# Pooled sums of the first batch by accumulated products on TensorE, with a new order of steps

## The chip, the cores and the metric

The kernel runs on one core of a Trainium2 chip (trn2). The metric is the time of one execution in device microseconds; a value for a kernel is the median of its runs. Engines are named as the profile names them: PE is TensorE (PEld its weight loads), DVE is VectorE, ACT is ScalarE, POOL is GpSimd, SP is SyncE, which issues all the transfers here.

## The reference, cut to what matters

Eight batches, eight heads, 576 tokens, head size 64. Attention has two parts that are added. The pooled part works on means over four tokens:

```python
q_d = q.reshape(B, H, Sd, factor, D).mean(axis=3)     # factor = 4, Sd = 144
k_d = k.reshape(B, H, Sd, factor, D).mean(axis=3)
v_d = v.reshape(B, H, Sd, factor, D).mean(axis=3)
out_up = np.repeat(sm_attn(q_d, k_d, v_d), factor, axis=2)
# local part: full q, k, v with a mask |i - j| < 4, softmax, times v
x = (out_up + out_local).transpose(0, 2, 1, 3).reshape(B * S, H * D)    # 4608 x 512
h = x @ w_in                                     # 512 x 1024
solu = h * softmax(h)
ln = (solu - mean) / sqrt(var + 1e-6) * g_ln
out = ln @ w_out                                 # 1024 x 512
```

All inputs of the attention are float32; the two weight matrices come as 64-bit floats.

## The kernel before, in words

Heads are worked in pairs (two heads of 64 fill 128 partitions), so a batch has four pairs. For each pair q and k are brought to the layout "head size on partitions, tokens along the row" (`qT`, `kT`, 128x576), and the sums over four neighbouring tokens are formed from it (`qd_flat`, `kd`, 128x144; the mean's factor is folded into the softmax scale).

The first two batches (`EarlyBatch`) get that layout from TensorE: a load puts 6 consecutive tokens of a head into each of 96 partitions, and twelve products with an identity matrix (6 token positions, 2 heads; tiles `qp`, `kp`, line L557) turn them into PSUM. One copy, on ACT or DVE (L263 or L265), moves 128x576 to `qT` or `kT`, and `sums` (L419, a DVE reduction over groups of four) makes `qd_flat` and `kd`. The later batches use DVE transposes instead (L463, L467), followed by the same reductions.

From there: `Pooled` per pair (products `sd`, L788; row maxima `mxd`, L795; exponentials `pd`, L803; scaling by the reciprocal sum, L812; transposes `pdt`, L823; products `po`, L844), `Local` per two windows of 64 tokens (scores `sc`, L600 and L607; L620 to L645; transposes `plt`, L655; products `xp`, L665), or `PairOfLocals` in the later batches. Their results add up in `x`.

The feed-forward network runs over 36 tiles of 128 tokens. `xhl` splits x in two float32r parts (`xh` on ACT, L1017; `xl`, L1020); `ffn_in` makes `h` from 24 matmuls of 512 columns (L862), then row maximum `nmx` (DVE, L870), exponential (ACT, L874), product (DVE, L877), small steps on POOL (L882 to L926). The result goes to memory and comes back in turned blocks (`u`, `v`; L910, L942), is turned by DVE (L963), split into `uh` and `ul` (L969, L972), and `ffn_out` makes `o` from 24 more matmuls (L986). The weights are converted once from 64-bit floats, in 16 pieces (`w`, L364 to L412), on ACT, DVE and POOL, while the first two batches run.

What sets the order: every kernel step (one stretch between two `yield`s) has a number, and the table `ORDER` lists all numbers in the sequence in which they are issued; each engine then works through its own instructions in that sequence. The table `OTHER` lists the steps whose work goes to the second choice of engine: `engine(usual, instead)` gives ACT or DVE for copies, POOL or DVE for most other places. There are 24 filler steps, `keep_clock`, of two bf16 matmuls each (tiles `warm`, L1043), which compute nothing that is used.

## Time and profile before

| | |
|---|---|
| median of 3 runs | 589.33 us (589.28 to 589.5) |
| the profiled execution, its own time | 585.0 us |
| its span | 583.2 us |
| granted TensorE clock | 0.999 |
| busy: PE / DVE / ACT / POOL | 564.1 / 469.3 / 333.8 / 299.5 us |
| instructions: PE / DVE / ACT / POOL | 5852 / 779 / 750 / 447 |

The profiled execution took 4.3 us less than the median of the runs, and its span is 1.8 us shorter than its own time; differences found in the trace are added to the median. Busy time is the time covered by an engine's instructions. A PE matmul's end is modelled, so neighbouring matmuls overlap in the record, and a short wait inside a row of matmuls counts as busy: the distance between starts says more than the length.

### The profile page before, as it was taken

Reading aid. Unit: us, or ns where it says so; the run is one execution under the profiler, and the core shown is the slowest. Engines: PE = TensorE matmul, PEld = TensorE weight load, DVE = VectorE, ACT = ScalarE, POOL = GpSimd, SP = SyncE. Lnnn points to the kernel's source line nnn. Section 1 sums busy time; section 2 is a strip of 40 time slices with the busy share of each in tenths; the row PEclk is TensorE's granted clock in tenths of the full one; section 3 lists DMA queues with packets and bytes.
Section 4 is the critical chain, followed back from the end, with each engine's and each line's share of the span. In section 5 each row is a group of like instructions: output and inputs, shape, how many; then the busy total and the mean of one; then the engine's idle time right before and its main releaser. Section 6 shows DMA issues by size and latency. Waiting matters only on the chain.

```text
span 583.2 us, 15261 instructions
## 1 busy us (share of the span) xinstructions
PE 564.1 (97%) x5852; PEld 434.1 (74%) x5852; DVE 469.3 (80%) x779; ACT 333.8 (57%) x750; POOL 299.5 (51%) x447
## 2 busy tenths in 40 slices
PE   7899998999999999999999999999999999999996
PEld 3676666777787777877777777777787777788875
DVE  7989999898988879998977967899878877545541
ACT  4778678468546646565565753466445654444442
POOL 3657677957454745648533546356433752334120
PEclk9999999999999999999999999999999999999999
DMA  8997767787877888876867976766755145304230
GB/s 280 286 213 187 189 148 193 200 193 171 228 160 185 188 191 169 194 198 157 208 153 195 228 190 167 212 157 159 195 163 148 56 145 164 127 36 163 90 110 37
DMA packets 207113, 99.59 MB, mean 171 GB/s; under 512 B 163136, under 2 KB 193344, under 8 KB 207040
## 3 DMA queue, kind: packets, MB, share of 16 engines
q1 hardware_dynamic: 207040, 98.61, 66.3%
q8 instruction: 46, 0.75, 0.6%
q14 instruction: 27, 0.22, 0.1%
HBM read 65.54 MB, written 27.79 MB: 160 GB/s over the span
## 4 chain that ended last, share of the span: by engine, by line
PE 64%; DVE 14%; SPq 7%; DMA 5%; ACT 4%; issue 3%; POOL 2%; POOLq 0%; DVEq 0%
PE o L986 27%; PE h L862 25%; SPq L286 4%; DMA v<-u 3%; PE po L844 2%; PE sd L788 2%; PE xp L753 1%; PE pdt L823 1%; PE sc L607 1%; PE sc L695 1%; DVE w L375 1%; DVE qd_flat L419 1%; DVE nmx L870 1%; SPq L942 1%; DVE e L877 1%
## 5 line engine op out<-in xcount | busy, mean ns | idle before, releaser
L986 PE MATMUL o<-wo_h,uh 128*128 128x512 f32 x288 | 116.6, 405 | 1.5 <-ACT osb L993 0.8
L862 PE MATMUL h<-wi_h,xh 128*128 128x512 f32 x288 | 116.9, 406 | 0.8 <-DVE e L877 0.6
L862 PE MATMUL h<-wi_h,xl 128*128 128x512 f32 x288 | 114.1, 396 | 0.7 <-POOL xl L1020 0.7
L986 PE MATMUL o<-wo_l,uh 128*128 128x512 f32 x288 | 113.8, 395 | 0.0
L862 PE MATMUL h<-wi_l,xh 128*128 128x512 f32 x288 | 113.7, 395 | 0.0
L986 PE MATMUL o<-wo_h,ul 128*128 128x512 f32 x288 | 78.9, 395 | 0.0
L972 POOL TENSOR_TENSOR ul<-v,uh 128x512 fp32r<-128x512 f32 x40 | 51.9, 1297 | 42.8 <-ACT uh L969 41.6
L874 ACT ACTIVATE e<-h,nmx 128x1024 f32<-128x1024 f32 x36 | 40.2, 1116 | 49.1 <-DVE nmx L870 45.5
L986 PEld LDWEIGHTS o<-wo_h,uh 128*128 128x128 f32 x288 | 54.0, 188 | 16.8 <-ACT osb L993 1.5
L862 PEld LDWEIGHTS h<-wi_h,xh 128*128 128x128 f32 x288 | 54.1, 188 | 15.8 <-issue 2.9
L862 PEld LDWEIGHTS h<-wi_h,xl 128*128 128x128 f32 x288 | 54.1, 188 | 15.4 <-POOL xl L1020 2.1
L986 PEld LDWEIGHTS o<-wo_h,ul 128*128 128x128 f32 x288 | 54.0, 188 | 13.4 <-DVE ul L972 0.3
L870 DVE TENSOR_REDUCE nmx<-h 128x1 f32<-128x1024 f32 x36 | 43.8, 1216 | 24.2 <-PE h L862 24.2
L986 PEld LDWEIGHTS o<-wo_l,uh 128*128 128x128 f32 x288 | 54.1, 188 | 12.0
L862 PEld LDWEIGHTS h<-wi_l,xh 128*128 128x128 f32 x288 | 54.1, 188 | 11.9
L877 DVE SCALAR_TENSOR_TENSOR e<-h,e 128x1024 f32<-128x1024 f32 x36 | 43.8, 1217 | 14.2 <-ACT e L874 14.0
L969 ACT ACTIVATE uh<-v 128x512 fp32r<-128x512 f32 x70 | 42.9, 624 | 18.5 <-issue 7.1
L963 DVE STREAM_TRANSPOSE v<-v 128x512 f32<-128x512 f32 x70 | 46.4, 689 | 7.6 <-DMA v<-u 7.5
L993 ACT ACTIVATE osb<-o,s 128x512 f32<-128x512 f32 x36 | 24.6, 682 | 40.0 <-PE o L986 22.1
L1020 POOL TENSOR_TENSOR xl<-x,xh 128x512 fp32r<-128x512 f32 (+1 forms) x26 | 32.9, 1268 | 22.5 <-ACT xh L1017 22.2
L487 POOL TENSOR_TENSOR vs<-vs 72x512 f32<-72x512 f32 x24 | 31.9, 1328 | 17.5 <-DMA vs<-in_v_dram 9.0
L882 POOL TENSOR_SCALAR nmu<-su 128x1 f32<-128x1 f32 x36 | 8.1, 226 | 60.1 <-DVE e L877 57.2
(128 smaller groups left out, 1116.3 us busy)
## 6 DMA issues: line engine op xcount, KB each, us to landing
u<-e SPq DMA_DIRECT2D x35, 512.0 KB
v<-u SPq DMA_DIRECT2D x140, 128.0 KB
vs<-in_v_dram SPq DMA_DIRECT2D x32, 288.0 KB
out_dram<-osb SPq DMA_DIRECT2D x36, 256.0 KB
qm<-in_q_dram SPq DMA_DIRECT2D x96, 72.0 KB
km<-in_k_dram SPq DMA_DIRECT2D x96, 72.0 KB
vw<-in_v_dram SPq DMA_DIRECT2D x80, 64.0 KB
vw<-in_v_dram SPq DMA_DIRECT2D x40, 128.0 KB
```

The source lines that it names most:

```text
L286: nc.sync.dma_start(t[nm][Q * 32:Q * 32 + 32, pr], src[b, 2 * pr + par, :, dh * 32:dh * 32 + 32].rearrange("(k t) d -> t k d", t=32),)
L487: eng.tensor_tensor(out=vs[:, :, 0:2 * D], in0=vs[:, :, 0:2 * D], in1=vs[:, :, 2 * D:4 * D], op=ALU.add)
L862: nc.tensor.matmul(hps[:, n, :], src[:, cc, :], wt[:, cc, n * 512:(n + 1) * 512], start=(cc == 0 and src is xh and wt is wi_h), stop=(cc = ...
L870: nc.vector.tensor_reduce(out=nmx, in_=hf, op=ALU.max, axis=AX.X, negate=True)
L874: nc.scalar.activation(e, hf, AF.Exp, bias=nmx, scale=1.0, accum_out=se)
L877: nc.vector.scalar_tensor_tensor(out=e, in0=hf, scalar=1.0, in1=e, op0=ALU.mult, op1=ALU.mult, accum_out=su)
L963: nc.vector.transpose(vg, vg)
L969: nc.scalar.activation(uh, tp, AF.Copy)
L972: (usual if v is None else engine(usual, nc.vector)).tensor_tensor(out=ul, in0=tp, in1=uh.bitcast(F32), op=ALU.subtract)
L986: nc.tensor.matmul(o, src[:, j, :], wt[:, 4 * g + j, :], start=(g == 0 and j == 0 and src is uh and wt is wo_h), stop=(g == 1 and j == 3 a ...
L993: nc.scalar.activation(osb, o, AF.Copy, scale=s)
L1020: engine(nc.gpsimd, nc.vector).tensor_tensor(out=l, in0=src, in1=h.bitcast(F32), op=ALU.subtract)
```

## The change

For batch 0 (`POOLED_ON_PE = 1`) the sums over four tokens no longer come from DVE reductions. Behind the twelve products that turn q or k of a pair, 14 more products per q and per k (7 for each head) read the same stationary tiles, with slices of the identity as the moving operand, and accumulate into 144 further columns of the same PSUM bank: a token position whose tokens fall into two different sums for even and odd partitions writes columns of both. One small copy per q and per k (128x144, ACT or DVE) takes them to `qd_flat` or `kd`. Batch 1 and the later ones are untouched.

```diff
+    POOLED_ON_PE = 1
...
+                if self.by_pe:
+                    three = tp[:, 0, n:n + SD].rearrange("x (m j) -> x m j", j=3)
+                    turn = ident[0:self.TP, 0:self.TP].rearrange("p (m e) -> p m e", e=2)
+                    for at_t, (t, js, es) in enumerate((
+                        (0, (0, 2, 1), (0, 2)), (1, (0, 2, 1), (0, 2)),
+                        (2, (2, 3, 1), (1, 2)), (2, (0, 1, 1), (0, 1)), (3, (0, 3, 2), (0, 2)),
+                        (4, (1, 3, 1), (0, 2)), (5, (1, 3, 1), (0, 2)),
+                    )):
+                        for par in range(2):
+                            nc.tensor.matmul(
+                                three[rows(par), :, js[0]:js[1]:js[2]],
+                                self.qk[nm, pr][:, par, t],
+                                turn[:, :, es[0]:es[1]], start=at_t == 0, stop=at_t == 6,
+                            )
                 yield
...
-                yield
+                if self.by_pe:
+                    copy(
+                        engine(nc.scalar, nc.vector),
+                        self.qd[pr] if nm == "q" else self.kd[:, pr], tp[:, 0, n:n + SD],
+                    )
+                yield
+            if self.by_pe:
+                return
             sums(self.qd[pr], self.qT[:, pr])
             yield
             sums(self.kd[:, pr], self.kT[:, pr])
...
-            row(bt.pair_steps(pr), 6 if bt.b < EARLY else 4)
+            row(bt.pair_steps(pr), 6 if POOLED_ON_PE <= bt.b < EARLY else 4)
...
-7 192 160 6 193 194 24 195 196 197 161 162 25 163 164 8 165 198 199 166 168 167 169 170 176 12
+30 152 22 153 19 154 8 155 156 157 32 24 26 25 184 185 186 187 158 29 159 21 168 188
```

The last pair of lines stands for the tables: batch 0 has eight steps less, so all numbers shift, and both `ORDER` and `OTHER` are new for the whole program. The 24 filler steps and all transfers are still there, in other places. The changed kernel's lines are later by 2 in the turning products (L559) and by 23 behind `pair_steps`; the new products are L573.

How PE's start moves, from the second pair's k of batch 0 (`kp`) on. Before:

```order
L557 MATMUL kp_245<-ident,km_142 64x96 x12
L788 MATMUL sd_0_260<-kd_220,qd_flat 64x144 x6
L557 MATMUL qp_2_271<-ident,qm_141 64x96 x12
L557 MATMUL kp_289<-ident,km_142 64x96 x12
L1043 LDWEIGHTS ident_b
L1043 MATMUL warm_303<-ident_b 128x512
```

And after, the same place (`kp_261` is that k, `qp_2` the third pair's q):

```order
L559 MATMUL kp_261<-ident,km_129 64x96 x12
L573 MATMUL kp_261<-ident,km_129 64x48x2 x4
L573 MATMUL kp_261<-ident,km_129 64x48 x4
L573 MATMUL kp_261<-ident,km_129 64x48x2 x6
L811 MATMUL sd_0_289<-kd_244,qd_flat 64x144 x6
L1066 LDWEIGHTS ident_b
L1066 MATMUL warm_302<-ident_b 128x512
```

Each turning group of batch 0 now has 14 products behind it, ahead of the first `sd`. Ahead of the very first turning group there were seven filler steps and there are now three; ahead of the first matmul of `ffn_in` there were 16 and there are 15.

On DVE, the place of the first sums, before (`w_1`, `w_2` are weight pieces under conversion, `mxd_0` the first pair's row maxima):

```order
L375 SCALAR_TENSOR_TENSOR w_1_162<-stage,w_1_162 128x512
L419 TENSOR_REDUCE qd_flat<-qT_185 128x144
L419 TENSOR_REDUCE kd_220<-kT_186 128x144
L379 SCALAR_TENSOR_TENSOR w_1_162<-stage,w_1_162 128x512
L370 TENSOR_SCALAR w_2_172<-w_2_172 128x512
L375 SCALAR_TENSOR_TENSOR w_2_172<-w_2_165,w_2_172 128x512
L379 SCALAR_TENSOR_TENSOR w_2_172<-w_2_165,w_2_172 128x512
L795 TENSOR_REDUCE mxd_0_267<-sd_0_260 128x3
```

And after, ahead of the first `mxd` (which is now the second pair's):

```order
L379 SCALAR_TENSOR_TENSOR w_0_136<-stage,w_0_136 128x512
L265 COPY qT_148<-qp_0_178 128x576
L265 COPY qd_flat<-qp_0_178 128x144
L366 TENSOR_SCALAR w_4_238<-w_4_238 128x512
L370 TENSOR_SCALAR w_4_238<-w_4_238 128x512
L412 TENSOR_TENSOR wi_l<-w_0_136,wi_h 128x4x4x32
L375 SCALAR_TENSOR_TENSOR w_4_238<-w_4_206,w_4_238 128x512
L379 SCALAR_TENSOR_TENSOR w_4_238<-w_4_206,w_4_238 128x512
L265 COPY qT_148<-qp_1_150 128x576
L265 COPY qd_flat<-qp_1_150 128x144
L412 TENSOR_TENSOR wi_l<-w_4_238,wi_h 128x4x4x32
```

The reductions are gone from this place, and copies and weight steps that ACT and POOL had stand there instead.

## Prediction

> **What bounds the kernel now.** I read the page first, then the busy time of each engine by stage, then PE's instructions in order of time in the first stages, then the groups by form for prices.

> ```profile
> span 583.2 us, 15261 instructions
> PE 564.1 (97%) x5852; PEld 434.1 (74%) x5852; DVE 469.3 (80%) x779; ACT 333.8 (57%) x750; POOL 299.5 (51%) x447
> PE   7899998999999999999999999999999999999996
> DVE  7989999898988879998977967899878877545541
> ```

> PE is busy for 97% of the span, and its digits are below 9 only at the two ends and in one slice from 87 to 102 us. DVE is as full as PE in the first fifth and loosens afterwards. So the early part has two full engines, and the change moves work between exactly these two. I cut the span at four points: the end of the last turning group of batch 0 (24.20 us), the first matmul of `ffn_in` (57.29), the start of steady alternation of `h` and `o` (110.40) and the tail (565.22). The columns are the stretch, its length, then busy time and instructions by engine:

> ```profile
> 0.00:24.20 24.20, 19.27 (x250) 11.46 (x251) 20.13 (x40) 14.22 (x34) 10.55 (x16) 1.00 0.95 285
> 24.20:57.29 33.09, 29.55 (x648) 21.72 (x646) 30.36 (x61) 26.43 (x72) 22.77 (x21) 1.00 0.89 205
> 57.29:110.40 53.11, 50.49 (x737) 37.39 (x731) 51.94 (x91) 38.31 (x78) 41.82 (x44) 1.00 0.77 192
> 110.40:565.22 454.82, 452.12 (x4172) 354.06 (x4173) 363.83 (x587) 249.35 (x560) 223.27 (x364) 1.00 0.65 165
> 565.22:583.20 17.98, 12.62 (x57) 9.49 (x54) 3.01 (x5) 5.45 (x9) 1.12 (x4) 0.96 0.12 44
> ```

> The order in which they are busy is PE, PEld, DVE, ACT, POOL. Stage 3 is DVE's (51.94 of 53.11). Stage 4 is PE's alone: 452.12 of 454.82, so whatever shift exists at 110 us is still there at the end. The visible idle time of PE is 4.93 + 3.54 + 2.62 us in the first three stages, and only these 11.1 us, with what the fillers cover, can take up new PE work. PE's own rows there (start, length, what):

> ```profile
> 3.32 6.49 PE L1043 MATMUL warm<-ident_b 128*128 128x512 bf16 x14 [3.32 <-DVE ident_b L216]
> 9.75 1.21 PE L557 MATMUL qp<-ident,qm 96*64 96x96 f32 x24
> 10.89 0.60 PE L1043 MATMUL warm<-ident_b 128*128 128x512 bf16 x2
> 11.43 1.21 PE L557 MATMUL kp<-ident,km 96*64 96x96 f32 x24
> 14.56 1.16 PE L557 MATMUL kp<-ident,km 96*64 96x96 f32 x24
> 15.65 0.71 PE L788 MATMUL sd<-kd,qd_flat 64*64 64x144 f32 x12
> 21.08 0.71 PE L788 MATMUL sd<-kd,qd_flat 64*64 64x144 f32 x12
> 21.71 1.21 PE L557 MATMUL qp<-ident,qm 96*64 96x96 f32 x24
> 24.20 0.39 PE L600 MATMUL sc<-mask_b,ident_b 128*128 128x256 bf16 x2
> 28.69 0.33 PE L607 MATMUL sc<-kT,qT 64*64 64x64 f32 x4 [1.15 <-issue]
> 35.84 0.33 PE L788 MATMUL sd<-kd,qd_flat 64*64 64x144 f32 x1 [1.13 <-issue]
> 57.29 0.50 PE L862 MATMUL h<-wi_h,xh 128*128 128x512 f32 x1
> ```

> Each f32 product is two records, so a turning group of 12 products is 24.

> **The products added.** A turning group holds 15.65 - 14.56 = 1.09 us, for 12 x 96 = 1152 moving columns. The 14 new products are ten of 96 columns and four of 48: also 1152. By columns a new group costs 1.09 us; if each product cost the same whatever its width it would be 14/12 of that, 1.27. No row here has an output of stride three or 48 columns, so I keep 0.95 (a little under the column price, since they run on behind the turning group) to 1.27 and take 1.09, the row with the same stationary tile and the same columns. Eight groups: **+8.7 us of PE** (7.6 to 10.2), all ahead of 57 us.

> **The work that leaves DVE, and what comes in its place.** Prices, as groups by form (busy, mean ns):

> ```profile
> L419 DVE TENSOR_REDUCE qd_flat<-qT 128x144 f32<-128x576 f32 x32 | 23.4, 733 | 0.0
> L265 DVE COPY qT<-qp 128x576 f32<-128x576 f32 x1 | 0.7, 749 | 0.0
> L265 DVE COPY pdT<-pdt 72x288 f32<-72x288 f32 x15 | 6.6, 443 | 3.8 <-ACT pdT L263 3.6 <-PE pdt L823 0.3
> L263 ACT ACTIVATE pdT<-pdt 72x288 f32<-72x288 f32 x49 | 18.3, 401 | 30.0 <-PE pdt L823 22.9 <-DVE pdT L265 4.9 <-PE po L844 2.2
> L263 ACT ACTIVATE x<-po 128x576 f32<-128x576 f32 x3 | 1.9, 648 | 0.0
> L366 DVE TENSOR_SCALAR w<-w 128x512 f32<-128x512 f32 x10 | 5.2, 528 | 2.6 <-ACT w L364 2.6
> L412 DVE TENSOR_TENSOR wi_l<-w,wi_h 128x512 fp32r<-128x512 f32 x1 | 0.7, 685 | 0.0
> L639 DVE TENSOR_REDUCE sml<-pl 128x8 f32<-128x520 f32 x20 | 13.6, 679 | 0.7 <-ACT pl L636 0.7
> L643 DVE RECIPROCAL rsl<-sml 128x8 f32<-128x8 f32 x20 | 4.1, 203 | 1.0
> L812 DVE TENSOR_TENSOR pd<-pd,rsd 128x432 f32<-128x432 f32 x12 | 7.3, 608 | 0.1
> L812 POOL TENSOR_TENSOR pd<-pd,rsd 128x432 f32<-128x432 f32 x20 | 19.0, 952 | 4.9 <-DVE rsd L810 4.0 <-DVE r L913 0.7
> L1020 DVE TENSOR_TENSOR xl<-x,xh 128x512 fp32r<-128x512 f32 x10 | 6.7, 676 | 2.4 <-ACT xh L1017 2.4
> ```

> Eight reductions leave: 8 x 0.733 = 5.9 us. A small copy of 144 columns lies outside the widths shown; on the line through 288 and 576 columns it is an estimate of 0.29 us on DVE (443 and 749) and 0.28 on ACT (401 and 648). Two of the eight go to DVE, six to ACT (+1.7 us, where stage 1 has ACT idle for 24.20 - 14.22 = 10 us, so I count it as nothing; without that cover it is at most the 1.7).

> But the order of the changed kernel refills DVE. I counted DVE's instructions ahead of the first `nmx` (the maximum of the first `h`). Against the eight reductions stand one more 576-column copy (0.749), two small ones (0.58), one more L366 (0.528), L412 (0.685), L639 and L643 (0.882), two more L812 (1.216) and an L1020 (0.676): 5.3 us. Net **-0.6 us of DVE** up to there. What the change frees on DVE goes into taking work from POOL (seven L812 ahead of the first tile become three). POOL's share of that, four times 0.952, is off the path in stages 1 and 2, where POOL has 10.55 and 22.77 us of work.

> **Stage 1.** After, the last turning group of batch 0 and its products need, in PE's order: the wait to 3.32; three slow fillers, 6 x (9.75 - 3.32)/14 = 2.8; eight turning and eight new groups, 16 x 1.09 = 17.4; three later fillers at 11.43 - 10.89 = 0.54 each, 1.6; two `sd` groups at 21.71 - 21.08 = 0.63, 1.3. Sum 26.4 us if nothing waits, against 24.20 now. The fillers show that PE begins slow: 0.46 us for a filler matmul in the first stretch, 0.27 later. With three fillers instead of seven, the slow time (to about 8 us) reaches into the first pair's groups; if they run at 0.46/0.27 of their length in it, that is about +1 at most. I take 27.0: **+2.8 us** (+1 if the slow fillers were the only reason PE was late, +4 with waits for the third pair's loads).

> [...]

> **Stage 2.** In the order between the last turning group of batch 0 and the first `h`, PE has one more `sd` group (+0.63) and four more fillers (8 instead of 4, +2.2). Fillers in a gap cost nothing, and DVE, 30.36 busy of 33.09, leaves such gaps; with no cover they cost 2.2. I take **+0.6** (-3.5 if all of PE's visible idle time goes, to +2.8). The two waits on "issue", 1.15 and 1.13 us, are 256 instructions apart. The changed PE has 448 more early (112 products, each two loads and two matmuls), so one or two such waits more, 0 to 2.3 us; I put them in the range. [...]

> **Stage 3.** Between the first and the fourth `nmx` DVE has 78 instructions before and 74 after. At 51.94/91 = 0.57 us each that is -2.3; I take **-2.0**, since DVE sets this stage. PE has 0.5 us more there and would hide it in its 2.6 us of idle time. In the new order `in3` also stands ahead of `out0`, which delays only the first output.

> **Stages 4 and 5.** PE's remaining work is unchanged, its tail order too, and DVE and POOL have a fifth and a half of the time free. **0** (-1 to +3, for an order that meets its transfers differently).

> Sum: +2.8 + 0.6 - 2.0 = +1.4 us. The profiled 585.0 would be 586.4, the median 589.33 + 1.4 = **590.7 us**. What a measurement of this kernel can tell from no change is 0.2%, 1.2 us.

> **The rivals.** First, faster. The chain of waits from 84 us on runs over POOL:

> ```profile
> 84.62 1.62 POOL wo_l L412
> 86.24 1.45 POOL pl L645
> 89.51 1.31 POOL ul L972
> 92.83 1.29 POOL xl L1020
> ```

> If steps taken from POOL shorten such chains, PE's gaps of stage 2 close: +2.2 (stage 1 dense, no slow group), +0.6 - 3.5 (stage 2), -2.3 (stage 3) = -3.0, 586.3 us. It decides from the point where stage 2 gives back over 2 us. For it speaks that DVE no longer sits between turning and `sd`; against it that 2.28 of the stage's 3.54 us of visible gaps are the issue waits, which no engine's relief closes. Chance 0.30, from 585 to 588.1.

> Second, no difference: stage 2 gives back half of its gaps (-1.8), and the rest stays as in my sum: +2.8 + 0.6 - 1.8 - 2.0 = -0.4, 588.9. This is also where it ends if the change doesn't act at all because fillers merely give way to products. Chance 0.23.

> Third, a long slow start: PE, with half as many fillers and narrow products, stays at its slow pace through the first six groups (6 x 1.09 = 6.5 more): 590.7 + 6.5 = 597. Against it, in before the turning groups from 9.75 on hold their pace with waits between them. Chance 0.07. [...]

> **How the numbers follow.** My forecast, slower by 1.2 to 5 us, has 0.40; with the slow start, slower has 0.47. Same 0.23, faster 0.30. The range 585.8 to 594.5 leaves out the slow start, the far end of the faster case and the sum with both issue waits and all of stage 4's +3: together just under 0.2. The likeliest case's own range is 590.5 to 594.5.

> **What would show it.** Right: new groups of about 1.09 us; the first `h` near 60 to 61 us rather than 57.29; DVE's first `nmx` right behind it; a fourth `nmx` some 53 to 55 us after the first matmul of `h`; PE idle in stage 4 near 2.7 us. Wrong: the first `h` at or ahead of 57 us, PE without visible gaps before it, or a stage 4 with several microseconds of new waits on DVE or POOL.

## Result, and the profile after

The changed kernel takes 589.91 us in the median (586.36 to 595.9, 20 runs), the kernel before 587.26 us (583.36 to 591.52, 20 runs); the ratio is 1.0059, 95% interval 1.0034 to 1.0084. It is slower, by 2.0 to 4.9 us of the 587 us. The runs of either kernel spread over 1.4 and 1.6%, only partly with their mean granted clock (0.990 to 0.999 in the changed kernel), and the ratios, here and below, are taken from the fast runs alone and are not the quotients of the medians. The profiled execution after took 587.59 us (585.0 before), so the two traces differ by 2.6 us, as the medians do.

The page of the changed kernel:

```profile
span 585.8 us, 15681 instructions
PE 571.4 (98%) x6076; PEld 443.9 (76%) x6076; DVE 469.3 (80%) x777; ACT 331.5 (57%) x746; POOL 302.4 (52%) x453
PE   7889999999999999999999999999999999999996
DVE  5989999999999898888889786989888666644541
```

PE has 7.3 us more of busy time, and between 44 us and the last slice none is below 9 any more; DVE's total is unchanged at 469.3 us. By stages, cut at the same events as before, but with two borders moved to instructions that are easy to find in both: the fourth `nmx`, and the last matmul of `h`. Columns: stretch, length, busy time of PE, PEld, DVE, ACT, POOL with instructions, granted clock, DMA share, GB/s. After:

```profile
0.00:26.93 26.93, 23.25 (x452) 18.56 (x452) 19.73 (x39) 14.11 (x37) 6.16 (x14) 1.00 0.92 263
26.93:63.77 36.84, 33.27 (x668) 24.20 (x667) 33.55 (x62) 26.94 (x73) 22.07 (x21) 0.91 0.78 202
63.77:116.39 52.62, 51.18 (x731) 38.07 (x729) 51.68 (x91) 37.54 (x79) 39.77 (x41) 1.00 0.83 181
116.39:561.76 445.37, 445.12 (x4165) 348.90 (x4158) 357.91 (x579) 245.22 (x547) 231.80 (x371) 1.00 0.66 167
561.76:585.80 24.04, 18.62 (x82) 14.22 (x80) 6.41 (x10) 7.69 (x12) 2.57 (x9) 1.00 0.14 49
```

Before, the three stretches whose borders moved:

```profile
57.29:111.65 54.36, 51.74 (x742) 38.42 (x737) 53.19 (x93) 39.52 (x80) 43.07 (x46) 1.00 0.76 190
111.65:559.23 447.58, 444.88 (x4142) 348.23 (x4140) 358.89 (x579) 245.79 (x554) 220.51 (x356) 1.00 0.65 166
559.23:583.20 23.97, 18.61 (x82) 14.30 (x80) 6.69 (x10) 7.81 (x12) 2.64 (x10) 0.97 0.17 55
```

(The prediction's third border was 110.40 us, 1.25 us ahead of this one.)

| stage | before | after | difference | predicted |
|---|---|---|---|---|
| to the last turning group of batch 0 | 24.20 | 26.93 | +2.73 | +2.8 |
| to the first `h` | 33.09 | 36.84 | +3.75 | +0.6 |
| to the fourth `nmx` | 54.36 | 52.62 | -1.74 | -2.0 |
| to the last `h` | 447.58 | 445.37 | -2.21 | 0 |
| to the end | 23.97 | 24.04 | +0.07 | 0 |
| sum | 583.20 | 585.80 | +2.60 | +1.4 |

PE's rows (start, length, what; in brackets the wait ahead and who ended it) hold the first two stages:

```profile
6.42 1.21 PE L559 MATMUL qp<-ident,qm 96*64 96x96 f32 x24
7.47 1.23 PE L573 MATMUL qp<-ident,qm 96*64 96x96 f32 x28
8.53 1.16 PE L559 MATMUL qp<-ident,qm 96*64 96x96 f32 x24
...
26.93 0.71 PE L811 MATMUL sd<-kd,qd_flat 64*64 64x144 f32 x12
30.82 0.86 PE L846 MATMUL pdt<-ident,pd 64*72 64x64 f32 x12 [3.18 <-DVE pd L835]
...
32.15 1.14 PE L630 MATMUL sc<-kT,qT 64*64 64x64 f32 x32
...
37.59 0.69 PE L630 MATMUL sc<-kT,qT 64*64 64x64 f32 x32
```

A group of 14 products takes 8.53 - 7.47 = 1.06 us. Then comes a wait that the kernel before did not have: 3.18 us for the first pair's scaled exponentials. Behind it a score group spans 1.14 us, and the same group 0.69 from 37.59 on. The clock rows around it:

```profile
30.00:31.00 1.00, 0.18 (x4) 0.21 (x6) 0.97 (x3) 0.00 (x0) 0.00 (x0) 0.68 1.05 279
31.00:37.00 6.00, 6.00 (x112) 3.82 (x113) 4.16 (x7) 3.83 (x14) 1.90 (x2) 0.50 1.11 252
37.00:38.00 1.00, 1.00 (x45) 0.69 (x41) 0.59 (x1) 0.56 (x2) 0.59 (x1) 0.91 0.82 214
```

The granted clock is 0.50 for 6.8 us in all (30.4 to 37.2), the end of the wait included. Of these PE worked from 30.82 on, 6.4 us at half pace: about 3.2 us lost. In this trace that is as much as stage 2's surprise. PE's visible idle time there is the same as before (3.57 us against 3.54: the wait took the place of the two waits on "issue"), while its busy time rose by 3.7 us.

What made `pd` late stands in DVE's rows, and in the first and last row of the six of POOL in that time, which follow each other without a pause:

```profile
22.70 1.11 DVE L366 TENSOR_SCALAR w<-w 128x512 f32<-128x512 f32 x1 [0.16 <-ACT w L364]
23.84 1.01 DVE L370 TENSOR_SCALAR w<-w 128x512 int32<-128x512 int32 x1
24.89 1.65 DVE L375 SCALAR_TENSOR_TENSOR w<-w,w 128x512 int32<-128x512 int32 x1
26.46 0.95 DVE L366 TENSOR_SCALAR w<-w 128x512 f32<-128x512 f32 x1
27.44 1.37 DVE L370 TENSOR_SCALAR w<-w 128x512 int32<-128x512 int32 x1
28.85 1.10 DVE L375 SCALAR_TENSOR_TENSOR w<-w,w 128x512 int32<-128x512 int32 x1
...
30.07 0.61 DVE L835 TENSOR_TENSOR pd<-pd,rsd 128x432 f32<-128x432 f32 x1
```

```profile
22.25 1.27 POOL L412 TENSOR_TENSOR wi_l<-w,wi_h 128x512 fp32r<-128x512 f32 x1 [19.88 <-ACT wi_h L410]
...
28.61 0.79 POOL L490 TENSOR_TENSOR vd<-vs 72x256 f32<-72x256 f32 x1
```

Six weight steps ahead of the scaling take 7.2 us. Where POOL is busy for less than half of the time, the same three forms take 0.42, 0.42 and 0.69 us (20, 31 and 31 rows in the first 70 us of four traces, of before, after and the second and third experiment; none over 0.70); twice that would be 3.1 us. The 4.1 us more exceed the wait of 3.18 us. The first experiment below takes three of the six steps out of the way: from the start of the second `sd` group to the end of this scaling it takes 10.3 us instead of 13.4.

Finally the later part. From 124 to 565 us, before and then after (two traces, one row each):

```profile
124.00:565.00 441.00, 438.30 (x4067) 343.34 (x4067) 351.50 (x567) 240.33 (x539) 213.88 (x349) 1.00 0.65 164
```

```profile
124.00:565.00 441.00, 440.75 (x4083) 345.56 (x4075) 352.03 (x569) 240.31 (x532) 225.81 (x363) 1.00 0.65 166
```

PE idles 2.70 us there before and 0.25 after. The new table gives back 2.4 us in a part that I had written down as unchanged.

### The profile page after: what moved, and what is told of

Read it like the earlier page. It is cut to its first block, busy times and chain, and to the rows that moved or that the text cites. A ratio compares the mean times of both kernels' runs of the same rounds, so it can differ in the third digit from the quotient of the medians.

```text
span 585.8 us, 15681 instructions
## 1 busy us (share of the span) xinstructions
PE 571.4 (98%) x6076; PEld 443.9 (76%) x6076; DVE 469.3 (80%) x777; ACT 331.5 (57%) x746; POOL 302.4 (52%) x453
## 4 chain that ended last, share of the span: by engine, by line
PE 88%; DVE 7%; ACT 2%; issue 1%; POOL 1%; DVEq 0%; POOLq 0%; ACTq 0%
PE o L1009 34%; PE h L885 33%; PE po L867 3%; PE sd L811 3%; PE pdt L846 2%; PE xp L776 2%; PE sc L630 2%; PE sc L718 2%; PE warm L1066 2%; PE xp L688 1%; PE plt L678 1%; PE qp L559 1%; PE kp L559 1%; DVE w L375 1%; DVE w L366 1%
## 5 line engine op out<-in xcount | busy, mean ns | idle before, releaser
L995 POOL TENSOR_TENSOR ul<-v,uh 128x512 fp32r<-128x512 f32 x36 | 47.0, 1306 | 35.0 <-ACT uh L992 33.6
L885 PEld LDWEIGHTS h<-wi_h,xl 128*128 128x128 f32 x288 | 54.1, 188 | 13.4 <-POOL xl L1043 0.3
L1009 PEld LDWEIGHTS o<-wo_h,ul 128*128 128x128 f32 x288 | 53.9, 188 | 13.4 <-DVE ul L995 0.3
L992 ACT ACTIVATE uh<-v 128x512 fp32r<-128x512 f32 x70 | 43.0, 624 | 30.4 <-DVE v L986 21.3
L1043 POOL TENSOR_TENSOR xl<-x,xh 128x512 fp32r<-128x512 f32 (+1 forms) x29 | 34.3, 1187 | 28.6 <-ACT xh L1040 28.5
L905 POOL TENSOR_SCALAR nmu<-su 128x1 f32<-128x1 f32 x36 | 9.6, 266 | 65.2 <-DVE e L900 56.5
L942 ACT ACTIVATE e<-e 128x1024 f32<-128x1024 f32 x35 | 36.7, 1049 | 9.5 <-DMA u<-e 9.4
```

What stands on the lines that cost most here:

```text
L885: nc.tensor.matmul(hps[:, n, :], src[:, cc, :], wt[:, cc, n * 512:(n + 1) * 512], start=(cc == 0 and src is xh and wt is wi_h), stop=(cc = ...
L942: nc.scalar.activation(e0, e, AF.Square, accum_out=m2)
L992: nc.scalar.activation(uh, tp, AF.Copy)
L995: (usual if v is None else engine(usual, nc.vector)).tensor_tensor(out=ul, in0=tp, in1=uh.bitcast(F32), op=ALU.subtract)
L1009: nc.tensor.matmul(o, src[:, j, :], wt[:, 4 * g + j, :], start=(g == 0 and j == 0 and src is uh and wt is wo_h), stop=(g == 1 and j == 3 a ...
L1043: engine(nc.gpsimd, nc.vector).tensor_tensor(out=l, in0=src, in1=h.bitcast(F32), op=ALU.subtract)
```

## Experiments

Three questions: is the slow clock behind the wait the price of stage 2; what do products and order each cost; and is the gain of the later part in the new table itself, or does any table catch up a late start? The first four kernels separate products, order and wait.

**The scaling first.** The changed kernel with the DVE steps `w5.1` to `w5.3` of the weight piece 5 moved behind the first pair's scaling (`w5.4` stood behind it already); `P_b0_2.1` is the third pair's row maxima, next behind it.

```diff
-ORDER ... w5.1 ... w5.2 ... w5.3 ... w5.4 ... P_b0_2.1 ...
+ORDER ... P_b0_2.1 w5.1 w5.2 w5.3 w5.4 ...
```

> The changed kernel with four DVE steps of weight piece 5 moved behind the scaling of the first pair's pd and the third pair's maxima. In the changed kernel PE stands still for 3.18 us at 27.6 us for that scaling, and then runs from 30.8 to 37.3 us at a granted clock of 0.50. Theory (the wait and the clock that falls in it make the loss of stage 2): the wait shrinks below 1 us, the clock stays at 1.00, the score groups last 0.63 instead of 1.07 us, the first matmul of h comes at 57.5 to 59 instead of 63.77, and the kernel ends 3 to 5 us earlier than the changed one, ratio to before 0.998 to 1.001. Rival (PE's 8.7 us of added products are the loss, and the wait only shows where there was room): the first h comes 1 us earlier at most, ratio 1.004 to 1.007.

Measured: 590.97 us, ratio 1.0067 [1.0029, 1.0105], no gain: the rival's ratio, though its reason is not thereby shown. The profiled execution took 599.15 us, 8 us above the median of the 12 runs, and its first `h` comes at 71.85 us. Two places in it tell something. First, PE's start, in which most of those 8 us arise:

```profile
6.43 2.19 PE L566 MATMUL qp<-ident,qm 96*64 96x96 f32 x24
...
20.50 2.06 PE L566 MATMUL kp<-ident,km 96*64 96x96 f32 x24
22.40 1.23 PE L580 MATMUL kp<-ident,km 96*64 96x96 f32 x28
```

The turning and product groups ran at half pace to 22.4 us, although PE's stream there is the same as in the changed kernel, and the first `sd` comes at 23.55 us instead of 16.11. Second, the waits of the first 75 us:

```profile
PE sc L637 <- issue: 1.1, 1, 1.1
PE pdt L853 <- DVE pd L842: 0.6, 1, 0.6
```

The wait for `pd` is down to 0.6 us, as meant, but one of 1.8 us for `pl` and one of 1.1 on "issue" follow at 39.0 to 42.8 us, and the clock falls there instead, again for 6.8 us. One of the 12 runs had a mean clock of 1.000 and took 585.93 us; the others had 0.990 to 0.997. So the wait is the first of a row, and in this execution removing it alone moved the fall.

**The new order with the old sums.** The new order and its engine choices, the sums by DVE reductions again, no products.

```diff
-                if self.by_pe:
+                if False:
                     three = tp[:, 0, n:n + SD].rearrange("x (m j) -> x m j", j=3)
...
-                    copy(
-                        engine(nc.scalar, nc.vector),
-                        self.qd[pr] if nm == "q" else self.kd[:, pr], tp[:, 0, n:n + SD],
-                    )
+                    sums(self.qd[pr] if nm == "q" else self.kd[:, pr], dst)
```

> The changed kernel's order with the sums of batch 0 back on DVE: no added products, and in the place of each small copy a DVE reduction from the turned q or k. PE has 8.7 us less, DVE 8 x 0.73 - 2 x 0.30 = 5.3 us more, ACT 1.7 us less. Theory (the products' PE time is paid at the end only where PE has no gap; DVE sets stages 1 to 3): the first h comes 0 to 3 us later than in the changed kernel, since DVE's chain to the first scaling is longer, ratio to before 1.003 to 1.010. Rival (PE work is the loss): the end comes 5 to 8 us earlier than the changed kernel's, ratio 0.993 to 0.998. Both expect stage 4, from the second o to the last h, near the changed kernel's 451 us and not the 455 of before, if that gain lies in the order.

Measured: 591.58 us, ratio 1.0082 [1.0049, 1.0114], as the theory said. The new order alone (with its engine choices) is slower than the old, with 8.7 us less PE work than the changed kernel. Its waits:

```profile
PE pdt L843 <- DVE pd L832: 5.5, 1, 5.5
PE sd L808 <- DVE kd L419: 3.4, 1, 3.4
```

DVE is late with the sums and with the scaling, the first `h` comes at 67.23 us, and the clock is at 0.50 from 20.1 us for 20.5 us. The mean clock of all 12 runs was 0.980 to 0.988 (median 0.997 in the runs of the kernel before). So 8.7 us less of PE work gain nothing in this order. Whether the products gain anything in it (1.0059 against 1.0082) the two intervals don't tell.

**The products in the old order.** Products and small copies as in the changed kernel, the table of before, the eight reductions' steps left empty.

```diff
+        by_pe = property(lambda self: self.b < 1)
...
+                if self.by_pe:
+                    three = tp[:, 0, n:n + SD].rearrange("x (m j) -> x m j", j=3)
...
-            sums(self.qd[pr], self.qT[:, pr])
+            if not self.by_pe:
+                sums(self.qd[pr], self.qT[:, pr])
```

> The kernel before, in its old order, with the sums of batch 0 by the added products and small copies at the turning steps; the eight DVE reductions are gone and nothing takes their place. PE +8.7 us, DVE -5.9 + 0.3, ACT +2.0. Theory (PE is the tighter engine of stage 1): the last turning group of batch 0 ends 4 to 6 us later than 24.2, the first h 2 to 5 us later than 57.3, ratio to before 1.003 to 1.008, with stage 4 at the 455 us of before. Rival (DVE is the tighter engine up to 110 us, and the relief counts where it is not refilled): the fourth nmx comes 3 to 5 us earlier than 111.4, ratio 0.992 to 0.996.

Measured: 595.06 us, ratio 1.0158 [1.0102, 1.0214]: the theory's side, but more than any of its numbers. The mean clock of the profiled run is 1.000, so this is the cleanest view of the products by themselves:

```profile
31.00 0.39 PE L623 MATMUL sc<-mask_b,ident_b 128*128 128x256 bf16 x2
...
63.19 0.50 PE L885 MATMUL h<-wi_h,xh 128*128 128x512 f32 x1
```

The first score group starts 6.8 us later (24.20 before), the first `h` 5.9 us later. The 8 x 1.06 = 8.5 us of products meet about 2 us of gaps, and DVE's 5.9 us of relief buys at most 0.9 us more by the first `h`: PE is the tighter engine there. From 124 us on PE idles 4.6 us instead of 2.7, so the loss grows again to 8.1 us at the last `nmx`.

**Fillers in the wait.** The changed kernel with four filler steps ahead of the first `pdt`.

```diff
+            if b == 0 and pr == 0:
+                for extra in range(4):
+                    keep_clock(100 + extra)
             pt = two_banks(ps_a, "a", f"pdt_{b}_{pr}")
```

> The changed kernel with four filler steps more (eight bf16 matmuls), right ahead of the transposes for which PE waits 3.18 us. The wait for DVE stays, but PE is busy in it for 4 x 0.54 = 2.2 us. Theory (the idle stretch makes the granted clock fall, and that costs 3.2 us by itself): the clock stays at 1.00, the score groups last 0.63 us, the transposes start at 30.8 as before, the first h comes at 60 to 61 instead of 63.77, and the kernel ends 2.5 to 3.5 us earlier than the changed one, ratio to before 1.000 to 1.002. Rival (the clock's fall lies beside DVE's work and costs nothing): the first h stays within 1 us of 63.8, ratio 1.004 to 1.007.

Measured: 591.29 us, ratio 1.0061 [1.0019, 1.0102], so again no gain. Locally it did part of what it should:

```profile
32.18 0.53 PE L849 MATMUL pdt<-ident,pd 64*72 64x64 f32 x12 [1.18 <-DVE pd L835]
...
38.16 0.56 PE L630 MATMUL sc<-kT,qT 64*64 64x64 f32 x19 [1.47 <-issue]
...
40.30 2.14 PE L559 MATMUL qp<-ident,qm 96*64 96x96 f32 x24
```

The wait shrank to 1.18 us and the score groups behind it ran at full pace (0.63 us a group). Then PE, now running through its instructions without a pause, met a wait of 1.47 us on "issue", and the clock fell there, for 3.4 us. The first `h` comes at 65.84 us, later than in the changed kernel; this execution too began at half pace, to 9.9 us. And five of the 12 runs had a mean clock of 0.999 or more, yet took 586.52 to 590.07 us, where nine runs of the kernel before beside them with such a clock took 583.62 to 586.88: keeping the granted clock up did not bring the kernel before's time. (One of the 12 took 629.11 us at a clock of 0.854.) "Issue" waits of this stage stand at the same place of PE's stream in several kernels: 1207 to 1209 records of PE and its loads lie ahead of it in seven of the experiments, 951 and 697 ahead of the two of the kernel before; that is 256 from one to the next, to within a missing record or two.

The next four tested order against fill. The two crossings share the theory on the later part.

**New start, old rest; and old start, new rest.** The changed program (products) with a table made of one order up to the first step of the fourth tile's `ffn_in` and of the other from there.

```diff
-ORDER = one table
+ORDER = one table up to in3.0 + the other steps in the sequence of the other table
```

> The changed kernel, in its own order of steps up to the first step of the fourth tile's ffn_in (about 105 us), and from there on in the order of the kernel before; nearly the same steps lie ahead of that point in both. Theory (the later part of the new table is itself shorter by what the trace showed behind 116 us, 3.6 us): the start keeps its loss, the gain is gone, 593 to 594 us, ratio to the kernel before 1.011 to 1.013. Rival (a late start is caught up behind 116 us by any order, since PE's waits there are for transfers and buffers that a late PE finds ready): as the changed kernel, 590, 1.006.

> The other half of the crossing: the products in the order of the kernel before up to the first step of the fourth tile's ffn_in, then the new order. Theory (the later part of the new table is shorter by itself): the 595.1 us of the old order with products, less 3.6 to 6, so 589 to 591.5, ratio 1.004 to 1.008. Rival (any order catches up what it can): 595, 1.015.

Measured: 601.68 us, ratio 1.0206 [1.0147, 1.0265], and 601.92 us, 1.0261 [1.0219, 1.0302]. Both miss every number. Their fourth `nmx` comes at 130.6 and 129.8 us, 14.2 later than in the changed kernel and 12.4 later than in the old order with products. Of this 7 and 4 us were lost ahead of the third `nmx` (a start at half pace to about 21.5 us in the first, a wait of 2.5 us on "issue" with a clock fall of 3.4 us in the second), 7 and 8 at the seam. The profiled execution of the first took 607.32 us, 5.6 above its median. Of the second crossing:

```profile
118.08 1.12 PE L695 MATMUL xp<-plT,vw 64*64 64x56 f32 x32 [5.99 <-ACT plT L270]
```

A wait of 6 us, with the clock at half for 10.2 us from within it on. At that seam half a weight piece and several steps of the local part lie on different sides in the two tables. That this makes the loss is a guess; these runs don't decide between theory and rival on the later part.

**More fillers at the start.** As the scaling first, with four fillers moved ahead of the first turning group, so seven there, and two added ahead of the first `pdt`.

```diff
-ORDER ... warm8 ...
+ORDER ... warm8 warm18 warm3 warm1 warm14 ...
...
+            if b == 0 and pr == 0:
+                for extra in range(2):
+                    keep_clock(100 + extra)
             pt = two_banks(ps_a, "a", f"pdt_{b}_{pr}")
```

> The changed kernel with seven instead of three fillers ahead of the first turning group (four taken from later places), the steps of the fifth weight piece behind the second scaling (as in the first experiment) and two added fillers ahead of the first turned probabilities. Theory (the halved clock behind PE's early idle time is the larger part of the loss of stage 2, and the narrow products at the start don't hold the clock up): mean clock 0.998 or more in most runs, score groups at 0.63 us, the first h near 60 to 61 us, time 586 to 588, ratio 0.999 to 1.003. Rival (the fillers cost their own time, the clock falls elsewhere): 590 to 592, ratio 1.006 or more.

Measured: 594.35 us, ratio 1.0132 [1.0093, 1.0171]: the rival's side, and worse. The groups at the start ran at full pace (1.04 and 1.06 us for the first two), but from 9.68 us instead of 6.42, and then:

```profile
36.78 0.39 PE L630 MATMUL sc<-mask_b,ident_b 128*128 128x256 bf16 x2 [1.23 <-DVE pl L652]
...
38.85 0.92 PE L637 MATMUL sc<-kT,qT 64*64 64x64 f32 x23 [1.36 <-issue]
```

Two short waits within 3.3 us, and the clock is down for 10.2 us. All six runs had a clock of 0.989 to 0.991. Removing `pd`'s wait does not make stage 2 faster, since its next limits lie right behind: DVE (33.55 busy of 36.84 us) and the issue waits.

**Old order, fewer fillers at the start.** The products in the old order, with four of the seven start fillers moved to the stage that DVE sets.

```diff
-ORDER ... warm12 warm22 warm1 warm3 pair b0 p0.0 ...
+ORDER ... pair b0 p0.0 ... warm17 warm12 warm22 warm1 warm3 ...
```

> The products in the order of the kernel before (595.1 us), with four of the seven fillers ahead of the first turning group moved behind the sixteenth filler's neighbour in the stage that DVE sets, as the new order has only three there. Theory (with the products PE alone sets the first stage, and fillers at 0.46 us a matmul stand on its path): 8 x 0.46 = 3.7 us at most, 1.8 if the first load comes that late anyway, so 591.4 to 593.3, ratio 1.008 to 1.012. Rival (the fillers only cover the wait for the first load, or without them PE runs the first groups at half pace): 595 to 597, ratio 1.015 or more.

Measured: 595.9 us, ratio 1.015 [1.011, 1.019], against 1.0158 with seven: the rival.

```profile
7.33 2.19 PE L565 MATMUL qp<-ident,qm 96*64 96x96 f32 x24 [0.84 <-DMA qm<-in_q_dram]
9.28 2.27 PE L579 MATMUL qp<-ident,qm 96*64 96x96 f32 x28
```

The first group starts 2 us earlier and then runs at half pace, so that the first `sd` comes at 19.43 us instead of 19.05. What the fillers took there, the slow pace took without them.

Then the price of a hole by itself, on the kernel before.

**A hole, and the same hole filled.** Ahead of the first score group PE waits for a small transfer, without fillers ahead of it (`hole(0)`) and with six (`hole(6)`).

```diff
+    late = cpool.tile([P, 32], BF16, name="late")
+    def hole(fillers):
+        nc.scalar.dma_start(late, filler[:, 0:32])
+        for extra in range(fillers):
+            keep_clock(200 + extra)
+        o = ps_o.tile([P, 512], F32, tag="o", name="hole")
+        nc.tensor.matmul(
+            o.rearrange("p (a n) -> p a n", n=32), filler,
+            late.unsqueeze(1).broadcast_to([P, 16, 32]), start=True, stop=True,
+        )
...
+            if b == 0 and u == 0:
+                hole(0)
```

> The kernel before (sums on DVE, its own order) with one thing added: ahead of the first score group (24.2 us) PE has a filler matmul whose operand is a 128x32 transfer that ACT issues behind the last copy of k, so PE idles for about 3 us there, as it does in the changed kernel. Theory (an idle stretch of some 3 us halves the clock, and that costs more than the wait itself): the clock falls behind the hole for about 7 us, which is 3.4 us, on top of the 3 us of the hole less what later gaps take up: 590 to 593 us, mean clock 0.994 or less in most runs. Rival (the wait alone is paid): 588 to 590 us, clock as before.

> The same as the hole, with six filler steps (3.2 us) between the last turning group and the waiting matmul: PE is as late, but busy. Theory (the clock is what counts): the clock stays as in the kernel before, and the time is some 3 us below that of the hole, 588 to 590 us. Rival (being late is all that counts): the same as the hole within 1 us.

Measured: 603.91 us, ratio 1.0293 [1.0248, 1.0338], and 605.51 us, 1.0326 [1.0289, 1.0363]. The pair did not do what it was designed for, since the transfer's issue on ACT waited some 7 us:

```profile
37.47 0.61 PE L1057 MATMUL hole<-late,ident_b 128*128 128x512 bf16 x1 [13.23 <-DMA late<-ident_b]
```

Filled, 8.6 us of idle time were still left, and the clock was down in both when the score groups began (1.07 us a group, 0.63 at full pace). It can't price the clock. It shows something else: 13.7 us of delay at the first score group are 12.6 us at the first `h`.

**A short hole.** As above, but the operand is written by 14 small copies on ACT behind the last copy of k.

```diff
+        for _ in range(14):
+            copy(nc.scalar, late, ident[:, 0:16])
+        nc.tensor.matmul(o[:, 0:16], ident, late, start=True, stop=True)
```

> The kernel before with one small matmul ahead of the first score group that waits for 14 copies of 128x16 on ACT, which follow the last copy of k (25.2 us): a hole of about 3.5 us in PE, made without a transfer, since the hole made with one became 13 us long. Theory (an idle stretch of over 3 us halves the clock for 3.4 to 10 us afterwards): the granted clock falls within or right behind the hole, the score groups behind it take 1.07 us instead of 0.63, and the first h comes 4.5 to 7 us later than before (61.5 to 64 us): the hole, plus 1 to 3.4 for the clock. Rival (the hole alone is passed on, or taken up by the gaps behind it): score groups at 0.63 us, the first h at most 3.5 us later.

Measured: 595.99 us, ratio 1.0167 [1.0109, 1.0224].

```profile
28.54 0.61 PE L1056 MATMUL hole<-late,ident 128*128 128x16 f32 x2 [4.27 <-ACT late L263]
...
29.51 1.13 PE L609 MATMUL sc<-kT,qT 64*64 64x64 f32 x32
...
35.97 0.69 PE L609 MATMUL sc<-kT,qT 64*64 64x64 f32 x32
```

The hole is 4.3 us, and it brings the slow clock in a kernel that had none there: 0.50 from 27.9 for 6.8 us, score groups of 1.07 us from start to start. The first score group is 4.8 us late, the slow clock adds about 3, and yet the first `h` comes at 61.10 us, 3.8 late, between theory (61.5 to 64) and rival (60.8 at most): stage 2 of the old order took up 4 us, of them 2.3 by the two issue waits, which are gone. So the cause and its local price are shown (a hole of 4 us, 6 us of work at half pace); how much of it reaches the first `h` depends on the gaps behind it. The changed kernel has hardly any there (0.4 us of waits besides the 3.18). The 9.9 us by which the last `nmx` is late in this trace are not the price of the hole: 6 of them come behind the first `h`, with a second fall of the clock at 92.7 us and more idle time from 124 us on.

**The kernel before with the new rest.** No products, the old order to the fourth step of the fourth tile's `ffn_in`, then the new one.

```diff
-ORDER = table of before
+ORDER = table of before up to in3.3 + the other steps in the new sequence
```

> The kernel before with its sums on DVE and its own order up to the fourth step of the fourth tile's ffn_in, where the sets of steps issued so far differ least between the two orders (13 steps), and from there the new order. Theory (behind the seam the new table is about 2 us shorter, and the 12 us that the other crossings lost belonged to their seam, which had half a weight piece on either side): 584 to 586 us, ratio 0.995 to 0.999, clock as before. Rival (each table is good only as a whole): 592 us or more, a loss of some 10 us within 30 us of the seam.

Measured: 586.11 us (before: 585.69), ratio 1.0012 [0.9988, 1.0037]: no difference, between theory (0.995 to 0.999) and rival (592 us or more).

```profile
124.00:565.00 441.00, 440.55 (x4070) 345.36 (x4069) 350.47 (x565) 237.62 (x528) 223.78 (x361) 1.00 0.64 165
```

The rest of the table does what the theory said: PE idles 0.45 us there instead of 2.70. But the seam cost as much, a wait of 1.7 us of `sd` for ACT and a half clock of 3.4 us from 120.7 on. Idle time of PE in this stretch, over all profiles that reach it: with the old rest 2.70, 4.60 (products), 3.68 (fewer fillers), 3.55 (crossing), 7.20 and 6.21 (holes) and 6.07 us (short hole, the row below); with the new rest 0.25, 0.32, 0.80, 0.48, 0.94, 0.26 and 0.45 us.

```profile
124.00:565.00 441.00, 434.93 (x4064) 340.04 (x4055) 355.01 (x571) 241.74 (x547) 213.89 (x342) 1.00 0.69 164
```

So the later gain belongs to the new table, whether PE arrives early (this kernel) or late. The old rest catches nothing up either: where PE comes later, it mostly idles more there, for `pd`, `v`, `e` and `r` of DVE and POOL, perhaps because their places were right for its own start; that is not shown. No kernel tried is faster than the kernel before.

## Why the prediction was right or wrong

**Slower** was right, and +1.4 a little short: the interval of the ratio begins at +2.0 us. The sum hid two misses of opposite sign, +3.15 in stage 2 and -2.2 in stage 4, so that it came so near is luck. That 590.7 lies within 1 us of the measured 589.91 is luck once more: the 589.33 it started from is the median of the first three of the 20 runs of the kernel before, 2.1 us above the median of all. Of the signs named ahead, the price of a group held; the first `h` at 63.77 missed 60 to 61, and PE's idle time in the later part was 0.25 us and not near 2.7.

**The products, +8.7 us.** Right: 1.06 us a group against 1.09. By columns, not by instructions (1.27); what the output of stride three and the 48 columns add is under 0.1 us a group, since the turning groups beside it take 0.99 to 1.05. The small copy took 0.296 us on DVE (estimate 0.29).

**Stage 1, +2.8.** Right at +2.73, and dense as assumed: idle behind the first 3.33 us fell from 1.6 to 0.4 us. The slow-start term was a coin that fell well here: in this trace the first group runs at full pace after three fillers, in the three other profiles with the same start it did not, to 9.9, about 21.5 and 22.4 us, and the first `sd` came 1.3, 7.0 and 7.4 us later. The third rival, at 0.07, is thus real, and can cost more than its 6.5 us. How often it happens in the changed kernel's runs is open, since the clock column does not show it; but its seven runs with a mean clock of 0.994 took from 587.59 to 595.9 us, so something beside the granted clock moves them, and the slow start may have a share in the measured difference that these stages, of one execution, don't show.

**Stage 2, +0.6.** This is the step that failed, at +3.75. The work in it was right by what is left: 3.75 less 3.2 for the slow clock leaves 0.6. (The trace has nine fillers there against five, not eight against four; the difference is the same.) What was missing is the row of waits. I counted DVE's work as 0.6 us less ahead of the first `nmx` and stopped at the count; the busy time of DVE to the first `h` rose instead by 53.28 - 50.49 = 2.8 us, with as many instructions (101), since weight steps that met POOL took longer (in the six rows above, 4.1 us). I also asked what would be late next only for fillers and issue waits, and not for `pd`, which now stands behind six weight steps on DVE. And I reckoned with a slow PE only at the start: here a wait of 3.18 us brought 6.4 us of work at half pace.

The traces give no one length of wait at which the clock falls. It fell 2.7 us after the start of the wait of 3.18 us, 3.6 after that of the hole of 4.27 and 2.0 after that of the hole of 13.23. A fall also came behind waits of 1.1 to 1.8 us, singly or in pairs (six experiments above), and yet not behind each: the same wait passes without one in the kernel before and brings one, of 3.4 us, in the short hole's kernel:

```profile
88.74 0.69 PE L665 MATMUL xp<-plT,vw 64*64 64x58 f32 x32 [1.69 <-ACT plT L263]
```

```profile
92.58 1.06 PE L667 MATMUL xp<-plT,vw 64*64 64x58 f32 x32 [1.72 <-ACT plT L263]
```

So a short wait is no cover, and the length of a wait alone does not tell. At the start PE was at half pace for 15 us in the first crossing and for 16 with the scaling first.

**The issue waits, 0 to 2.3 us.** In the changed kernel they are gone from stage 2, as PE stands still for other reasons ahead of those places; where that wait is taken away, they return (1.1 to 1.5 us). So they look like a maximum with the other waits, and not like a term to be added to them.

**Stage 3, -2.0.** Right in size: -1.74, and -1.6 between the first and the fourth `nmx` (46.72 against 48.31 us), by fewer DVE instructions.

**Stages 4 and 5, 0.** Wrong at -2.2. "PE's remaining work is unchanged" held; that its 2.7 us of idle time would stay did not. I had the number in the quoted row of stage 4 and treated it as a floor.

**The rivals.** The faster case asked for stage 2 to give back over 2 us; it took 3.75. Without the slow clock the profiled difference would by these numbers be about -0.6 us, the no-difference case, but the runs don't bear that out: three of the 20 with a mean clock of 0.999 took 586.36, 586.45 and 590.53 us, and 26 runs of the kernel before with 0.999 or more, taken beside the experiments, took 582.15 to 587.73, with a median of 584.85. What the slow clock adds in the median is therefore open.

## What to carry to other kernels

Where a reordering puts a wait of a few microseconds into an otherwise dense engine, price the clock behind it, not only the wait (here 3.2 us lost behind a wait of 3.18), and look at what stands behind that wait before removing it. Count DVE's instructions with the time that they take beside a busy POOL (L366 here 0.77 us on average instead of 0.42). And a written-out order is right for the arrival times it was made for: read the idle time that the old one leaves in later stages as something that a new order can win or lose, and don't cut two orders together where steps are half done.

## What was not expected of the hardware

DVE's weight steps took longer beside a busy POOL. In the first 70 us of the four traces named above the weight steps of L366 and L370 (one input) took 0.42 us with POOL mostly idle, and 0.77 and 0.72 on average with POOL busy for over half of the time (15 and 14 rows, up to 1.51 and 1.37); L375 with two inputs 0.69 and 0.88 (12 rows, up to 1.65). Not every row is delayed: the six of L375 with POOL busy in the kernel before took 0.68 us on average. In the changed kernel's six rows above the delays are 0.4 to 1 us, beside POOL instructions of 0.8 to 1.4; what makes them, no trace shows.

```profile
6.00:22.00 16.00, 15.94 (x181) 13.70 (x181) 8.20 (x16) 3.47 (x7) 0.00 (x0) 1.00 1.04 272
```

This is the experiment with the scaling first. The pace of a group that is known from elsewhere, 1.05 us against 2.0, tells more than that column there.
